# Gated attention block in fp32r: the odd tile's output sum split by inner channels, one more mirrored half of a key pair, and u's load and turn moved

## The chip, the cores and the metric

The kernel runs on one core of a Trainium2 chip. The metric is the device time of one execution in microseconds, as the median of several runs. The engines are TensorE (PE, with PEld for its weight loads), VectorE (DVE), ScalarE (ACT), GpSimd (POOL) and SyncE (SP), whose queue issues nearly all DMA transfers here.

## The reference

For eight batches of 3200 positions, with 256 channels and 64 channels for the scores:

```python
scores = scale * np.matmul(z, z.transpose(0, 2, 1))   # scale = 1 / 3200
attn = np.maximum(scores, 0.0) ** 2
x = u * np.matmul(attn, v)
gate_pre = sum over k < 5 of conv_w[k] * (x shifted by 4 - k positions)
gate = 1 / (1 + exp(-gate_pre))
out = (gate * (x @ w_val)) @ w_out
```
The weights of the attention are symmetric, since queries and keys are the same `z`.

## The kernel before

All products are made of three fp32r matmuls: each operand is split into a high and a low part (`ah`, `al` for the attention's weights, `gvh`, `gvl` for the gated values), and low x high, high x low and high x high are added in PSUM. The high part is a cast, mostly on ACT, and the low part a subtraction on DVE.

A batch has 25 tiles of 128 positions. The queries go in 7 chunks of 4, 4, 4, 4, 3, 3, 3 tiles (the last batch: 4, 4, 4, 4, 4, 3, 2); the keys in 13 pairs of tiles, of which the last is single. A *step* is one pair of one chunk, 91 steps to a batch, and the program is written step by step. In step s TensorE multiplies the values with the weights of step s (`attend`, lines 338 and 532), and makes the scores of step s + 3 (`AHEAD`), from which ACT (relu, square, cast; lines 489, 490, 492) and DVE (`al`, line 498) make that step's weights. The order on each engine is the order in which the program writes it; a table `todo` says after which step each piece of side work stands (`at_step`).

*Mirrored pairs.* Where the scores of an earlier chunk already hold the block, transposed, it isn't computed again: DVE turns blocks of the weights (`turned`, line 413, two buffers), SP writes them to DRAM (`mir`), and a later chunk fetches them (`m<-mir`, `m_fetch`, four buffers) three steps before they are cast. `mirrored` asks that both tiles of the pair are kept. Pair 9 (tiles 18 and 19) lies across chunks 4 and 5 in all batches but the last: for the queries of chunk 5, tile 18's block is kept, tile 19 is its own chunk. So far the whole pair is computed there.

*Behind the attention.* When a chunk is done, DVE multiplies the accumulators with the turned `u` (`gated`, line 562, `x<-acc,ut`). During the next chunk the convolution, the gate and the value product follow (`BEHIND`), with `gvl` of the inner channels 0 to 127 (`e = 0`) at step 8 and of 128 to 255 (`e = 1`) at step 11. At the first step of the chunk after that comes the output projection (`project`, or `project_whole` where no scores are due in the step): two banks `misc0` and `misc1`, whose even tiles go to the one and odd tiles to the other. Of the last tile of an odd chunk each bank gets half the output channels (`project_places`). ACT copies bank 0 after step 1 and bank 1 after step 2 into `ob` (`out_copy`, line 724), which SP stores.

*u.* SP loads `u` of a chunk as eight transfers in four groups, one group a step (`u_load`), and DVE turns it (`u_prep`, line 551, `ut<-u_raw`). There is one buffer of each, so a load waits until the turn of the chunk before is done. The steps are counted from the first of the chunk that it belongs to: loads begin at -6 in chunks 0, 1 and 6 and at -11 in the others, and the turn stands at 1.

Of the kernel before, what the change touches and what calls it, by code (L numbers as in the profile page):

```python
# [11 lines left out]
ALU = mybir.AluOpType  # L12
P = 128
BLK = 32
# [3 lines left out]
def attn_glu_kernel(  # L18
# [345 lines left out]
    def scores(b, c, i, terms=range(3)):  # L364
# [13 lines left out]
        for j in range(2):  # L378

            g, t = all_homes[b][k + (j if n == 2 else 0)]  # L380
            ks = slice(t * P, (t + 1) * P)
            qs = slice(0, a) if n == 2 else slice(j * (a // 2), (j + 1) * (a // 2))
            kk = zt[b, g]
            mms = []
            for m in terms:
                kp, qp = ((0, 1), (1, 0), (0, 0))[m]
                mms.append((s[:, j, : w * n // 2], kk[:, kp, ks], q[:, qp, qs], m == 0, m == 2))
            sides.append(mms)
# [9 lines left out]
    def halves(b, c, i):  # L398
        return two_pairs(b, c) and i == own(b, c, 1)

    def mirrored(b, c, i):
# [37 lines left out]
    def m_fetch(b, c, i):  # L439

        n, y = pairs[i][1], all_sizes[b][c] * BLK
        mt = m_in[b, c, i] = sb.tile([P, 2 * CW], F32, name="m", bufs=4)
        if halves(b, c, i):
            nc.sync.dma_start(mt[:, : 16 * BLK], mirror[b, c, c].rearrange("p a x -> p (a x)"))
            return
        into = mt[:, : P // BLK * n * y].rearrange("p (a x) -> p a x", x=n * y)
        for j, g, t, m in runs(b, i):
            nc.sync.dma_start(into[:, :, j * y : (j + m) * y], mirror[b, g, c][:, :, t * y : (t + m) * y])
# [6 lines left out]
    def weights_of(b, c, i):  # L455
# [5 lines left out]
        hi, lo = ah[:, : n * w], al[:, : n * w]  # L461
        if halves(b, c, i):
            s = st_.pop((b, c, i))
            a = sb.tile([P, 2 * CW], F32, name="a", bufs=2)[:, :w]
            nc.scalar.activation(a.rearrange("p (j x) -> p j x", j=2), s[:, :, : w // 2], AF.Relu, scale=scale)
            nc.scalar.activation(a, a, AF.Square)  # L466
            m = m_in.pop((b, c, i))[:, :w].rearrange("p (a j x) -> p a j x", a=P // BLK, j=2)

            his, los = (x.rearrange("p (j a h x) -> p a j h x", j=2, a=P // BLK, h=2) for x in (hi, lo))
            a = a.rearrange("p (j a x) -> p j a x", j=2, a=P // BLK)  # L470
            parts = [(m, his[:, :, :, 0], los[:, :, :, 0])]
            parts.append((a, *(x[:, :, :, 1].rearrange("p a j x -> p j a x") for x in (his, los))))
            for src, h, _ in parts:
# [188 lines left out]

    def project_places(b, c):

        n = all_sizes[b][c]
        whole, half = slice(0, D), D // 2
        banks = [[], []]
        for t in range(n - n % 2):
            banks[t % 2].append((t // 2 * D, t, whole))
        if n % 2:  # L670
            for x in range(2):
                banks[x].append((n // 2 * D, n - 1, slice(x * half, (x + 1) * half)))
        return banks

    def project_list(b, c, x, first, last):
        wh, wl = weights["out"]
        gvh, gvl = gvs[b, c]
        places = project_places(b, c)[x]
        out_ = []
        for e in range(DH):  # L680
            for p, (at_, t, ch) in enumerate(places):
                ts = slice(t * P, (t + 1) * P)
                po = pos[b, c][x][:, at_ : at_ + ch.stop - ch.start]
                for m, (gp, wp) in enumerate(((gvl, wh), (gvh, wl), (gvh, wh))):
                    out_.append(
                        (
                            po,
                            gp[:, e, ts],
                            wp[:, e, ch],
                            first and e == p == m == 0,  # L690
                            last and e == DH - 1 and p == len(places) - 1 and m == 2,
                        )
                    )
        return out_
# [24 lines left out]
    def out_copy(b, c, x, on=nc.scalar.copy):  # L719
        if x == 0:  # L720
            obs[b, c] = sb.tile([P, CW // P, D], F32, name="ob", tag=OB.get((b, c), "gvl"), bufs=1)
        ob = obs[b, c]
        for at_, t, ch in project_places(b, c)[x]:
            on(ob[:, t, ch], pos[b, c][x][:, at_ : at_ + ch.stop - ch.start])

# [24 lines left out]
    def start(b, c):  # L750
# [20 lines left out]
    Z_FROM = {b: (-12, -7, -1, 7, 17, 23, 32) if b > 1 else (22, 26, 3, 8, 17, 30, 34) for b in range(1, B)}  # L771

    CONVERSIONS = (
        (2, 2, convert_conv(), 14),
# [3 lines left out]
    for b in range(B):  # L778
        for c in range(n_chunks):
            s0 = start(b, c)  # L780
            nxt = s0 + NP
            for h in range(DH):
                for part in range(2):
                    at_step((s0 - 11 if 1 < c < n_chunks - 1 else max(s0 - 6, 2)) + 2 * h + part, u_load, b, c, h, part)
            if (b, c) != LAST:
                for r, fn, args in BEHIND:
                    at_step(nxt + r, fn, b, c, *args)
                for x in range(DH):
                    at_step(nxt + project_at(*steps[nxt][:2]) + 1 + x, out_copy_before, b, c, x)
            at_step(max(s0 + 1, 6), u_prep, b, c)  # L790

# [18 lines left out]
            for i in range(NP):  # L810
                if mirrored(b, c, i) or halves(b, c, i):
                    at_step(s0 + place[b, c, i] - AHEAD - FETCH, m_fetch, b, c, i, first=True)
# [159 lines left out]
```

## Time and profile before

| | |
|---|---|
| median of 3 runs | 2310.14 us (2309.87 to 2310.98) |
| the profiled execution | 2310.52 us, its span 2308.7 us |
| granted TensorE clock | 1.000 |
| PE, PEld, DVE, ACT busy | 100%, 87%, 78%, 77% of the span |
| DMA | 465 MB, 76.2% of 16 engines' span on SP's queue |
| chain of waits, by engine | PE 95%, ACT 2%, DVE 1%, DMA 1%, issue 1% |

The busy share of PE is that of matmuls whose ends are modelled; they are pipelined, so the time that one takes from the next is the distance between two starts, which the timeline shows. A row of the timeline gives the start, the time (of all its instructions), engine and line, the operation, tiles and shapes, and in brackets the idle time before it with what ended it. A row of waits gives who waited for whom: total us, times, longest. A row of groups gives count, total busy time and mean ns, and then the idle time before them.

### The profile page before, as it was taken

What the parts mean: (1) busy time and instruction counts of PE and PEld (TensorE: products, weight loads), DVE (VectorE), ACT (ScalarE), POOL (GpSimd) and SP (SyncE); (2) the same over time, 40 slices, a digit from 0 to 9 for tenths busy, and PEclk for the clock granted to TensorE, in tenths of its full rate; (3) what the DMA queues carried; (4) which work ended last, traced back from release to release, by engine and by line L of the source; (5) the groups of instructions that cost most, each with busy time, mean ns of one, the idle gap of its engine ahead of it and who ended that gap; (6) DMA issues with size and microseconds to landing.
All of it is one profiled execution on the core that took longest, in us unless ns stands there. A gap on an engine that the chain in (4) does not pass through costs nothing.

```text
span 2308.7 us, 47650 instructions
## 1 busy us (share of the span) xinstructions
PE 2300.3 (100%) x18845; PEld 2019.1 (87%) x18845; DVE 1810.4 (78%) x2362; ACT 1782.7 (77%) x2417; POOL 55.0 (2%) x108
## 2 busy tenths in 40 slices
PE   9999999999999999999999999999999999999999
PEld 7889988889888998889988899888998889988889
DVE  8777787787878878788788887788877888778776
ACT  8988788776888768887688776887768876687765
POOL 0000000000000000000000000000000000000000
PEclk9999999999999999999999999999999999999999
DMA  6255798778977889688896789878897788976653
GB/s 132 65 157 154 204 260 206 197 202 238 249 187 202 216 237 249 168 212 220 239 235 182 202 226 245 220 190 207 236 229 209 206 215 229 249 179 165 182 165 90
DMA packets 684881, 465.04 MB, mean 201 GB/s; under 512 B 351600, under 2 KB 635504, under 8 KB 684656
## 3 DMA queue, kind: packets, MB, share of 16 engines
q1 hardware_dynamic: 683600, 461.86, 76.2%
q8 instruction: 148, 2.42, 0.5%
q14 instruction: 77, 0.63, 0.1%
q10 hardware_dynamic: 1056, 0.13, 0.0%
HBM read 250.36 MB, written 211.48 MB: 200 GB/s over the span
## 4 chain that ended last, share of the span: by engine, by line
PE 95%; ACT 2%; DVE 1%; DMA 1%; issue 1%; SPq 0%; DVEq 0%; ACTq 0%
PE acc L338 44%; PE acc L532 29%; PE s L338 10%; PE misc L338 6%; PE misc L706 5%; PE misc L640 1%; ACT a L490 1%; DMA v_hl<-v_kept 1%; ACT a L489 1%; ACT ah L492 0%; DVE gvl L661 0%; DMA mir<-turned 0%; DVE al L498 0%; SPq L166 0%; DMA z_raw<-in_z_dram 0%
## 5 line engine op out<-in xcount | busy, mean ns | idle before, releaser
L338 PE MATMUL acc<-ah,v_hl 64*128 64x512 f32 (+1 forms) x6632 | 1073.1, 375 | 0.4 <-DVE v_hl L296 0.4
L338 PEld LDWEIGHTS acc<-ah,v_hl 64*128 64x128 f32 x6632 | 620.6, 184 | 112.6 <-issue 13.0
L532 PE MATMUL acc<-ah,v_hl 128*128 128x384 f32 (+2 forms) x2284 | 639.0, 355 | 0.1
L498 DVE TENSOR_TENSOR al<-a,ah 128x1024 fp32r<-128x1024 f32 (+3 forms) x395 | 431.1, 1092 | 260.6 <-ACT ah L492 252.3
L338 PE MATMUL acc<-al,v_hl 64*128 64x512 f32 (+1 forms) x3316 | 626.7, 374 | 0.7 <-DVE al L498 0.7
L489 ACT ACTIVATE a<-s 128x1024 f32<-128x1024 f32 (+3 forms) x395 | 362.7, 918 | 194.2 <-PE s L338 191.3
L532 PEld LDWEIGHTS acc<-ah,v_hl 128*128 128x128 f32 x2284 | 416.8, 188 | 47.5 <-ACT a L466 7.1
L498 DVE TENSOR_TENSOR al<-m,ah 128x768 fp32r<-128x768 f32 (+2 forms) x303 | 307.9, 1023 | 134.4 <-ACT ah L492 133.7
L532 PE MATMUL acc<-al,v_hl 128*128 128x384 f32 (+2 forms) x1142 | 402.2, 352 | 0.0
L490 ACT ACTIVATE a<-a 128x1024 f32<-128x1024 f32 (+3 forms) x395 | 378.3, 958 | 12.6
L492 ACT CAST ah<-m 128x768 fp32r<-128x768 f32 (+2 forms) x303 | 267.3, 892 | 147.6 <-DMA m<-mir 98.0
L338 PEld LDWEIGHTS acc<-al,v_hl 64*128 64x128 f32 x3316 | 312.7, 184 | 47.6 <-DVE al L498 1.2
L492 ACT CAST ah<-a 128x1024 fp32r<-128x1024 f32 (+2 forms) x357 | 339.4, 951 | 11.3
L413 DVE STREAM_TRANSPOSE turned<-a 128x1024 f32<-128x1024 f32 (+3 forms) x318 | 319.3, 1010 | 8.2 <-DMA mir<-turned 6.7
L603 DVE SCALAR_TENSOR_TENSOR gate<-x,cw,gate 128x512 f32<-128x512 f32 (+2 forms) x448 | 303.5, 678 | 4.4 <-ACT gate L601 0.3
L338 PE MATMUL s<-zq,zhl 64*128 64x512 f32 (+3 forms) x2052 | 261.8, 358 | 0.0
L532 PEld LDWEIGHTS acc<-al,v_hl 128*128 128x128 f32 x1142 | 214.8, 188 | 14.9 <-DVE al L498 0.2
L338 PEld LDWEIGHTS s<-zq,zhl 64*128 64x128 f32 x2052 | 185.8, 184 | 29.5
L562 DVE TENSOR_TENSOR x<-acc,ut 128x512 f32<-128x512 f32 (+2 forms) x112 | 67.5, 629 | 41.8 <-PE acc L338 26.3
L608 ACT ACTIVATE gate<-gate 128x512 f32<-128x512 f32 (+2 forms) x112 | 65.4, 583 | 34.2 <-DVE gate L603 34.1
L304 ACT CAST v_made<-v_raw 128x512 fp32r<-128x512 f32 x97 | 55.9, 576 | 40.4 <-DMA v_kept<-v_made 39.4
L706 PE MATMUL misc<-w_out_hi,gvl 128*128 128x256 f32 (+1 forms) x304 | 85.8, 282 | 0.6 <-DVE gvl L661 0.3
(114 smaller groups left out, 2020.8 us busy)
## 6 DMA issues: line engine op xcount, KB each, us to landing
m<-mir SPq DMA_DIRECT2D x191, 384.0 KB, 5.1
mir<-turned SPq DMA_DIRECT2D x340, 192.0 KB, 3.7
mir<-turned SPq DMA_DIRECT2D x188, 256.0 KB, 4.3
m<-mir SPq DMA_DIRECT2D x94, 512.0 KB, 6.0
v_hl<-v_kept SPq DMA_DIRECT2D x84, 512.0 KB, 6.7
v_kept<-v_made SPq DMA_DIRECT2D x71, 512.0 KB, 5.1
u_raw<-in_u_dram SPq DMA_DIRECT2D x264, 64.0 KB, 3.7
out_dram<-ob SPq DMA_DIRECT2D x33, 512.0 KB, 4.0
```

The source lines that it names most:

```text
L304: nc.scalar.copy(v_made[b, g, t][:, 0, :m, :], v_raw[b, g][:, t : t + m, :])
L338: ins = nc.tensor.matmul(out_, st[r], mv[r], start=first, stop=last)
L413: nc.vector.transpose(into[:, t : t + m], a[:, j * w : (j + m) * w].rearrange("p (t m x) -> p t m x", t=m, x=BLK))
L489: nc.scalar.activation(a.rearrange("p (j x) -> p j x", j=2), s[:, :, :each], AF.Relu, scale=scale)
L490: nc.scalar.activation(a, a, AF.Square)
L492: nc.scalar.copy(hi, a)
L498: nc.vector.tensor_tensor(lo, a, f32(hi), op=ALU.subtract)
L532: nc.tensor.matmul(out_, st, mv, start=first, stop=last)
L562: nc.vector.tensor_tensor(x[:, h, HALO : HALO + w], accs[b, c][h][:, :w], ut[b, c][:, h, :w], op=ALU.mult)
L603: nc.vector.scalar_tensor_tensor(g, tap, cw[:, h, k : k + 1], g, op0=ALU.mult, op1=ALU.add)
L608: nc.scalar.activation(g, g, AF.Sigmoid)
L706: nc.tensor.matmul(out_, st, mv, start=first, stop=last)
```

## The change

There are three parts.

1. The last tile of an odd chunk is projected with all 256 output channels into both banks: bank 0 gets the sum over the inner channels `e = 0`, bank 1 that over `e = 1`. ACT copies bank 0's part, and DVE adds bank 1's. The list of matmuls now also goes tile by tile within `e`.
2. Pair 9 of chunk 5 (`split`): tile 18's weights are fetched from the mirror, and only tile 19 is computed, its queries divided between the two row halves of TensorE.
3. In batches 1 to 7 `u` is loaded from -2 on in chunks 1 and 2 and from -9 in chunk 3, and turned at step 10 in chunks 0 and 1 and at step 3 in chunk 2.

```diff
+            one_tile = n == 1 or split(b, c, i)
+            g, t = all_homes[b][k + (n - 1 if one_tile else j)]
-            qs = slice(0, a) if n == 2 else slice(j * (a // 2), (j + 1) * (a // 2))
+            qs = slice(j * (a // 2), (j + 1) * (a // 2)) if one_tile else slice(0, a)
...
+    def split(b, c, i):
+        (j, g, *_), *more = runs(b, i)
+        return bool(more) and more[0][1] == c and keeps(b, g, c) and (b, c) != (B - 1, n_chunks - 1)
...
-        for j, g, t, m in runs(b, i):
+        for j, g, t, m in runs(b, i)[: 1 if split(b, c, i) else None]:
+            if split(b, c, i):
+                into = mt[:, : P // BLK * y].rearrange("p (a x) -> p a x", x=y)
...
-        if halves(b, c, i):
+        if halves(b, c, i) or split(b, c, i):
...
+            m = m_in.pop((b, c, i))[:, :w]
+            if split(b, c, i):
+                parts = [(m, hi[:, :w], lo[:, :w]), (a, hi[:, w:], lo[:, w:])]
...
-        places = project_places(b, c)[x]
+        places = [(t, e) for e in range(DH) for t in range(x, n - n % 2, 2)] + [(n - 1, x)] * (n % 2)
+        for p, (t, e) in enumerate(places):
+            ts = slice(t * P, (t + 1) * P)
+            po = pos[b, c][x][:, t // 2 * D : (t // 2 + 1) * D]
+            for m, (gp, wp) in enumerate(((gvl, wh), (gvh, wl), (gvh, wh))):
+                ends = p == len(places) - 1 and m == 2
+                out_.append((po, gp[:, e, ts], wp[:, e], first and p == m == 0, last and ends))
...
+        for t in range(x, n - n % 2, 2):
+            on(ob[:, t, :], pos[b, c][x][:, t // 2 * D : (t // 2 + 1) * D])
+        if n % 2:
+            half = pos[b, c][x][:, n // 2 * D : (n // 2 + 1) * D]
+            if x == 0:
+                nc.scalar.copy(ob[:, n - 1, :], half)
+            else:
+                nc.vector.tensor_tensor(ob[:, n - 1, :], half, ob[:, n - 1, :], op=ALU.add)
...
+    U_LOAD = ((-6, -6, -11, -11, -11, -11, -6), (-6, -2, -2, -9, -11, -11, -6))
+    U_PREP = ((1,) * n_chunks, (10, 10, 3) + (1,) * (n_chunks - 3))
...
-                    at_step((s0 - 11 if 1 < c < n_chunks - 1 else max(s0 - 6, 2)) + 2 * h + part, u_load, b, c, h, part)
+                    at_step(max(s0 + U_LOAD[b > 0][c], 2) + 2 * h + part, u_load, b, c, h, part)
...
-            at_step(max(s0 + 1, 6), u_prep, b, c)
+            at_step(max(s0 + U_PREP[b > 0][c], 6), u_prep, b, c)
```

How this moves instructions, at three places. First TensorE, the projection of chunk 4 of batch 2 at the start of chunk 6, where bank 0's list ends and bank 1's begins. Before:

```order
L706 MATMUL misc0_11564<-w_out_hi_1008,gvl_11335 128x256
L706 MATMUL misc0_11564<-w_out_lo_1009,gvh_11334 128x256
L706 MATMUL misc0_11564<-w_out_hi_1008,gvh_11334 128x256
L706 MATMUL misc0_11564<-w_out_hi_1008,gvl_11335 128x128
L706 MATMUL misc0_11564<-w_out_lo_1009,gvh_11334 128x128
L706 MATMUL misc0_11564<-w_out_hi_1008,gvh_11334 128x128
L706 MATMUL misc1_11565<-w_out_hi_1008,gvl_11335 128x256
L706 MATMUL misc1_11565<-w_out_lo_1009,gvh_11334 128x256
L706 MATMUL misc1_11565<-w_out_hi_1008,gvh_11334 128x256
```
Now:

```order
L700 MATMUL misc0_11516<-w_out_hi_1008,gvl_11285 128x256
L700 MATMUL misc0_11516<-w_out_lo_1009,gvh_11284 128x256
L700 MATMUL misc0_11516<-w_out_hi_1008,gvh_11284 128x256
L700 MATMUL misc1_11517<-w_out_hi_1008,gvl_11285 128x256
L700 MATMUL misc1_11517<-w_out_lo_1009,gvh_11284 128x256
L700 MATMUL misc1_11517<-w_out_hi_1008,gvh_11284 128x256
```
A bank had two groups of three wide and three narrow matmuls, one for each `e`; now it has three groups of three wide ones, in bank 0 for tile 0 with `e = 0`, tile 0 with `e = 1` and tile 2 with `e = 0`.

Second ACT, chunk 5 of batch 2 at pair 9. Before:

```order
L608 ACTIVATE gate_11164<-gate_11164 128x384
L492 CAST ah_11298<-m_11209 128x4x2x96
L489 ACTIVATE a_11341<-s_11314 128x768
L490 ACTIVATE a_11341<-a_11341 128x768
L492 CAST ah_11339<-a_11341 128x768
L656 CAST gvh_11334<-gv_11336 128x384
```
Now:

```order
L620 ACTIVATE gate_11112<-gate_11112 128x384
L504 CAST ah_11248<-m_11157 128x4x2x96
L473 ACTIVATE a_11291<-s_11264 128x384
L474 ACTIVATE a_11291<-a_11291 128x384
L486 CAST ah_11289<-m_11179 128x384
L486 CAST ah_11289<-a_11291 128x384
L668 CAST gvh_11284<-gv_11286 128x384
```
The two passes have half the elements, and the cast has become two of half the size, the first from the fetched block `m`.

Third DVE at the end of chunk 1 of batch 2, from the last pair's `al` (of halves) to the accumulators. Before:

```order
L652 TENSOR_TENSOR gv_9406<-misc1_9160,gate_8933 128x512
L479 TENSOR_TENSOR al_9421<-m_9253,ah_9420 128x4x2x64
L479 TENSOR_TENSOR al_9421<-a_9422,ah_9420 128x8x64
L498 TENSOR_TENSOR al_9448<-m_9305,ah_9447 128x4x2x128
L661 TENSOR_TENSOR gvl_9256<-gv_9406,gvh_9255 128x512
L562 TENSOR_TENSOR x_9473<-acc0_8899,ut_8986 128x512
```
Now:

```order
L664 TENSOR_TENSOR gv_9343<-misc1_9099,gate_8877 128x512
L491 TENSOR_TENSOR al_9358<-m_9190,ah_9357 128x4x2x64
L491 TENSOR_TENSOR al_9358<-a_9359,ah_9357 128x8x64
L563 STREAM_TRANSPOSE ut_9381<-u_raw_8746 128x1024
L510 TENSOR_TENSOR al_9387<-m_9242,ah_9386 128x4x2x128
L673 TENSOR_TENSOR gvl_9193<-gv_9343,gvh_9192 128x512
L574 TENSOR_TENSOR x_9415<-acc0_8843,ut_9381 128x512
```
The turn of chunk 1's `u` stood behind `xl` at the chunk's step 1; now it stands between the last pair's `al` and the next chunk's first. On SP the eight loads of chunk 2's `u`, which stood among the writes of chunk 1's turned blocks, now stand in a row behind the last fetch for chunk 2 and ahead of the store of an output.

More of the change, by code (lines that the diff above doesn't have):

```diff
@@ L378, in scores @@
         for j in range(2):
-            g, t = all_homes[b][k + (j if n == 2 else 0)]
+            one_tile = n == 1 or split(b, c, i)
+            g, t = all_homes[b][k + (n - 1 if one_tile else j)]
             ks = slice(t * P, (t + 1) * P)
-            qs = slice(0, a) if n == 2 else slice(j * (a // 2), (j + 1) * (a // 2))
+            qs = slice(j * (a // 2), (j + 1) * (a // 2)) if one_tile else slice(0, a)
             kk = zt[b, g]
@@ L386, in scores @@
                 kp, qp = ((0, 1), (1, 0), (0, 0))[m]
-                mms.append((s[:, j, : w * n // 2], kk[:, kp, ks], q[:, qp, qs], m == 0, m == 2))
+                mms.append((s[:, j, : w // 2 if one_tile else w], kk[:, kp, ks], q[:, qp, qs], m == 0, m == 2))
             sides.append(mms)
@@ L466, in weights_of @@
             nc.scalar.activation(a, a, AF.Square)
[L467 to L472, printed above, removed]
+            m = m_in.pop((b, c, i))[:, :w]
+            if split(b, c, i):
+                parts = [(m, hi[:, :w], lo[:, :w]), (a, hi[:, w:], lo[:, w:])]
+            else:
+                m = m.rearrange("p (a j x) -> p a j x", a=P // BLK, j=2)
+                his, los = (x.rearrange("p (j a h x) -> p a j h x", j=2, a=P // BLK, h=2) for x in (hi, lo))
+                a = a.rearrange("p (j a x) -> p j a x", j=2, a=P // BLK)
+                parts = [(m, his[:, :, :, 0], los[:, :, :, 0])]
+                parts.append((a, *(x[:, :, :, 1].rearrange("p a j x -> p j a x") for x in (his, los))))
             for src, h, _ in parts:
@@ L661, in gate_value_low, with project_list @@
         nc.vector.tensor_tensor(gvl[:, e, :w], gv_.pop((b, c, e))[:, :w], f32(gvh[:, e, :w]), op=ALU.subtract)
-    def project_places(b, c):
+    def project_list(b, c, x, first, last):
         n = all_sizes[b][c]
[L666 to L675, printed above, removed]
         wh, wl = weights["out"]
         gvh, gvl = gvs[b, c]
-        places = project_places(b, c)[x]
+        places = [(t, e) for e in range(DH) for t in range(x, n - n % 2, 2)] + [(n - 1, x)] * (n % 2)
         out_ = []
[L680 to L693, printed above, removed]
+        for p, (t, e) in enumerate(places):
[4 more added lines that the diff above has]
+                out_.append((po, gp[:, e, ts], wp[:, e], first and p == m == 0, last and ends))
         return out_
@@ L722, in out_copy @@
         ob = obs[b, c]
-        for at_, t, ch in project_places(b, c)[x]:
-            on(ob[:, t, ch], pos[b, c][x][:, at_ : at_ + ch.stop - ch.start])
+        n = all_sizes[b][c]
+        for t in range(x, n - n % 2, 2):
[4 more added lines that the diff above has]
+                nc.scalar.copy(ob[:, n - 1, :], half)
+            else:
+                nc.vector.tensor_tensor(ob[:, n - 1, :], half, ob[:, n - 1, :], op=ALU.add)
     def out_store(b, c):
@@ L810, in attn_glu_kernel @@
             for i in range(NP):
-                if mirrored(b, c, i) or halves(b, c, i):
+                if mirrored(b, c, i) or halves(b, c, i) or split(b, c, i):
                     at_step(s0 + place[b, c, i] - AHEAD - FETCH, m_fetch, b, c, i, first=True)
```

## The prediction

> **What bounds the kernel now.** I read the page first (busy shares, chain of waits), then TensorE's waits, then the timeline at the places that the change touches.
>
> ```profile
> PE 2300.3 (100%) x18845; PEld 2019.1 (87%) x18845; DVE 1810.4 (78%) x2362; ACT 1782.7 (77%) x2417; POOL 55.0 (2%) x108
> ```
> ```profile
> PE acc L338 <- DVE al L498: 0.7, 1, 0.7
> ```
> ```profile
> PEld misc L706 <- DVE gvl L661: 2.1, 7, 0.5
> ```
> PE is busy for 2300.3 of 2308.7 us. A busy PE need not be fast, so I looked at who holds it up: the second row (TensorE's waits) shows that a late `al` holds a matmul once in the whole run, and the third that a late `gvl` holds a weight load seven times, 2.1 us in sum. Starts of matmuls follow one another by their own length almost everywhere. So time goes or comes by what TensorE itself has to issue, as long as DVE, ACT and the transfers keep their lead.
>
> **The odd tile's projection.** An odd chunk (three tiles) has 12 matmuls of 256 columns and 12 of 128 columns now, and 18 of 256 after the change. First one whole projection row by row, up to the start of what follows it, then an even chunk's from the chain of waits (24 matmuls of 256).
>
> ```profile
> 841.28 0.28 PE L706 MATMUL misc<-w_out_hi,gvl 128*128 128x256 f32 x1
> ...
> 841.63 0.22 PE L706 MATMUL misc<-w_out_hi,gvl 128*128 128x128 f32 x1
> 841.69 0.28 PE L706 MATMUL misc<-w_out_lo,gvh 128*128 128x128 f32 x1
> 841.80 0.27 PE L706 MATMUL misc<-w_out_hi,gvh 128*128 128x128 f32 x1
> 841.91 0.33 PE L706 MATMUL misc<-w_out_hi,gvl 128*128 128x256 f32 x1
> 842.09 0.28 PE L706 MATMUL misc<-w_out_lo,gvh 128*128 128x256 f32 x1
> ...
> 843.97 0.39 PE L532 MATMUL acc<-ah,v_hl 128*128 128x384 f32 x1
> ```
> ```profile
> 398.81 2.87 PE misc L706 x24
> ```
> From start to start a 256-column matmul takes 0.12 us (0.35 for the first three). The three of 128 columns take 0.06, 0.11 and 0.11, and the wide one behind them 0.18 in place of 0.12: the narrow ones are no cheaper than a wide one in practice. The whole takes 843.97 - 841.28 = 2.69 us. Eighteen wide ones at 2.87/24 = 0.1196 take 2.15. Saved: 0.54 per odd chunk.
>
> Where the projection runs on the two row halves at once, the timeline shows the same:
>
> ```profile
> 875.39 0.28 PE L338 MATMUL misc<-w_out_hi,gvl 64*128 64x256 f32 x2
> ...
> 876.71 0.45 PE L338 MATMUL s<-zq,zhl 64*128 64x512 f32 x2
> 877.00 0.33 PE L338 MATMUL misc<-w_out_hi,gvl 64*128 64x256 f32 x2
> ...
> 878.37 0.44 PE L338 MATMUL acc<-ah,v_hl 64*128 64x512 f32 x2
> ```
> 1.32 + 1.37 = 2.69 us again. How many there are follows from the groups of matmuls by form:
>
> ```profile
> L338 PE MATMUL misc<-w_out_hi,gvl 64*128 64x128 f32 x112 | 12.5, 219 | 0.0
> ```
> ```profile
> L706 PE MATMUL misc<-w_out_hi,gvl 128*128 128x128 f32 x32 | 7.1, 221 | 0.0
> ```
> A whole projection has 4 narrow matmuls with `gvl`, one on halves has 8, so 32/4 + 112/8 = 8 + 14 = 22 odd chunks. **Term 1: 22 x 0.54 = 11.9 us less.** The last of them (2296.64) lies straight ahead of the final chunk's value matmuls, so it counts too.
>
> A rule bears on this. The Trainium skill, TensorE: Matmul & The Clock Gate, section "Back-to-back issue gap", gives an isolated gap of N/2.4 + 2.5 ns, which is 56 ns for 128 columns and 109 for 256; by it 12 narrow ones cost what 6 wide ones cost, and term 1 would be an estimated 0.3 us in place of 11.9. The rows of 0.11 us do not agree with it. The page's section "LDWEIGHTS" puts a load of 128 columns at 107 ns, and with that they agree.
>
> The other side of term 1: the two sums are now added by one DVE instruction of 256 elements that reads PSUM, 22 times, while ACT loses two short copies and gains one of 256. The nearest row reads PSUM too:
>
> ```profile
> L562 DVE TENSOR_TENSOR x<-acc,ut 128x256 f32<-128x256 f32 x2 | 0.8, 420 | 1.0 <-PE acc L532 1.0
> ```
> That is 22 x 0.42 = 9.2 us of DVE. It stands at step 2 of a chunk, ahead of the `al` that TensorE needs at step 5. In chunk 1, the tightest of the three kinds that get it, that `al` ends 2.3 us before its first use:
>
> ```profile
> 653.75 1.22 DVE L498 TENSOR_TENSOR al<-a,ah 128x1024 fp32r<-128x1024 f32 x1 [0.68 <-ACT ah L492]
> ```
> ```profile
> 657.29 0.39 PE L338 MATMUL acc<-al,v_hl 64*128 64x512 f32 x2
> ```
> Since the turn of `u` (1.23 us) leaves the same stretch, I take nothing. Without cover it would be 9.2 us.
>
> A shorter projection is also a shorter cover: it runs while DVE empties the accumulators that the next chunk writes. At the start of chunk 6 the first of them is free at
>
> ```profile
> 842.19 0.55 DVE L562 TENSOR_TENSOR x<-acc,ut 128x384 f32<-128x384 f32 x1
> ```
> 842.74, and TensorE writes it at 843.97 (above). Of these 1.23 us, 0.54 go; 0.7 stay, so again nothing.
>
> **The pair across two chunks.** Seven times (batches 0 to 6, chunk 5, pair 9) six score matmuls of 384 columns become six of 192. Both sizes are in the trace, with the start of what follows:
>
> ```profile
> 826.66 0.68 PE L338 MATMUL s<-zq,zhl 64*128 64x384 f32 x6
> 827.18 0.33 PE L338 MATMUL acc<-ah,v_hl 64*128 64x384 f32 x2
> ```
> ```profile
> 834.46 0.47 PE L338 MATMUL s<-zq,zhl 64*128 64x192 f32 x6
> 834.77 0.36 PE L338 MATMUL acc<-ah,v_hl 64*128 64x384 f32 x2
> ```
> 0.52 against 0.31, **term 2: 7 x 0.21 = 1.5 us less.** ACT does two passes on half the elements and casts in two pieces; DVE subtracts in two pieces, some 0.1 us more. The seven added fetches of 192 KB are issued three steps ahead. One that came late would hold ACT first, and TensorE only beyond the lead of that pair's `al`, which ends at 830.93 and is used at 833.59:
>
> ```profile
> 829.97 0.96 DVE L498 TENSOR_TENSOR al<-a,ah 128x768 fp32r<-128x768 f32 x1 [3.83 <-ACT ah L492]
> ```
> ```profile
> 833.59 0.33 PE L338 MATMUL acc<-al,v_hl 64*128 64x384 f32 x2
> ```
> A lead of 2.7 us; I take nothing for the fetches.
>
> **u late.** For batches 1 to 7 the turn of `u` moves from step 1 to step 10 in chunks 0 and 1, from 1 to 3 in chunk 2, and the loads of chunks 1, 2 and 3 by 4, 9 and 2 steps. What DVE does around step 10 now:
>
> ```profile
> 632.81 1.23 DVE L498 TENSOR_TENSOR al<-m,ah 128x1024 fp32r<-128x1024 f32 x1 [1.63 <-ACT ah L492]
> ...
> 680.83 1.23 DVE L498 TENSOR_TENSOR al<-m,ah 128x1024 fp32r<-128x1024 f32 x1 [1.48 <-ACT ah L492]
> ```
> Directly ahead of these two (ends of chunks 0 and 1) DVE idles 1.63 and 1.48 us, and the moved turn of 1.23 stands exactly there: it costs nothing. In chunk 2 the loads are issued from about 686 on, where SP is idle (rows under rival C), for some 4 us, and land 3.7 us after issue (median on the page), at about 694. The turn now stands at
>
> ```profile
> 693.16 1.24 DVE L551 STREAM_TRANSPOSE ut<-u_raw 128x1024 f32<-128x1024 f32 x1
> ```
> and goes two steps, some 7 us, later: in time. Where the turn left in chunk 0, it frees time at the one `al` that TensorE waits for:
>
> ```profile
> 317.89 1.25 DVE L413 STREAM_TRANSPOSE turned<-a 128x1024 f32<-128x1024 f32 x1 [3.16 <-DMA mir<-turned]
> ...
> 319.90 1.23 DVE L551 STREAM_TRANSPOSE ut<-u_raw 128x1024 f32<-128x1024 f32 x1
> ...
> 321.49 1.22 DVE L498 TENSOR_TENSOR al<-a,ah 128x1024 fp32r<-128x1024 f32 x1
> ```
> ```profile
> 322.76 0.50 PE L338 MATMUL acc<-al,v_hl 64*128 64x512 f32 x2 [0.75 <-DVE al L498]
> ```
> Without the turn this `al` comes 1.2 us sooner. **Term 3: 0.8 us less** (the idle 0.75 and a slower restart), bounds 0 and 0.9.
>
> Sum: 11.9 + 1.5 + 0.8 = 14.2. The profiled execution took 2310.5 (2308.7 of span, 1.8 around it), so 2296.3; the median of the timed runs lies 0.4 lower, so **2295.9**.
>
> **Rivals.**
>
> *A: gvl of the second half comes late.* In the new order bank 0 reaches `e = 1` after three matmuls (0.36 us), so far after six (0.63). At the start of chunk 6 that `gvl` is just done, and at the start of chunk 5 (an even projection) it is the wait of the seven rows above:
>
> ```profile
> 841.12 0.55 DVE L661 TENSOR_TENSOR gvl<-gv,gvh 128x384 fp32r<-128x384 f32 x1
> ```
> It ends at 841.67, 0.39 us into the projection; TensorE would want it at 0.36. For it: that is late by 0.03 and a handshake, and the seven waits now cost 2.1/7 = 0.3 us each. Against it: chunk 5 is where the split pair takes work off ACT, which is busy nearly without a break from that pair to the end of the chunk. ACT's first pass on 768 and on 384 elements:
>
> ```profile
> 827.38 0.81 ACT L489 ACTIVATE a<-s 128x768 f32<-128x768 f32 x1 [4.21 <-PE s L338]
> ...
> 835.99 0.48 ACT L489 ACTIVATE a<-s 128x384 f32<-128x384 f32 x1
> ```
> 0.33 less on each of two passes, against 0.2 for the second piece of the cast: some 0.5, while TensorE gains 0.21. So `gvl` should come at about 0.39 - 0.5 + 0.21 = 0.1. Price if ACT's gain is lost: 0.39 + 0.21 - 0.36 = 0.24 late and some 0.14 of handshake and restart, 0.4 each, 7 times, 2.7 us: **2298.6**. Chance 0.13.
>
> *B: narrow matmuls cost only their columns*, and the 0.11 us comes from something else that stays (the accumulation in one bank, say). Then terms 2 and 3 alone remain: 2310.1 - 2.3 = **2307.8**. For it is only the first narrow one's 0.06. Chance 0.05.
>
> *C: u's loads block SP's queue, slower.* Eight issues now stand in a row at the ends of chunks 0 and 1, behind a wait for DVE's turn; the writes of the turned blocks are queued behind them, and a late write holds DVE as at 317.89. SP in chunk 2 now, and the issue time of two loads:
>
> ```profile
> 685.47 0.52 SPq L448 DMA_DIRECT2D m<-mir  x1
> 696.20 0.41 SPq L729 DMA_DIRECT2D out_dram<-ob  x1
> ...
> 700.36 0.99 SPq L166 DMA_DIRECT2D u_raw<-in_u_dram  x2
> ```
> Eight take 4.0 us. If all of it reached DVE, less the 2.3 us of lead, it is 1.7 us at each of 14 places, 24 us: **2320**. It decides from 14.2/14 = 1.0 us a place on. Against it: SP issues nothing from 686.0 to 696.2, just where the eight will stand. Chance 0.03.
>
> **How the numbers follow.** Forecast 0.79, A 0.13, B 0.05, C 0.03. The forecast's own range is 2294.5 to 2297.5 (term 3 at nothing, term 1 by 0.05 a chunk). With A, and half of the DVE adds' price showing in two of three kinds of chunk (some 3 us), the range is 2294.3 to 2300.8. A measurement of this kernel tells about 0.2%, 4.6 us, from no change: faster by that is forecast and A (0.92), B is no change (0.05), C slower (0.03).
>
> **What would show it.** Right: an odd projection of 2.15 us, in both forms; the split pair's scores in 0.31; `ut` of chunks 0 and 1 in DVE's idle time just before the last `al` of the chunk, with no wait for its transfer; no PE wait at batch 1, chunk 0; DVE's `ob` add not in the chain. Wrong: waits of `misc` for `gvl` more than seven (A), odd projections near 2.6 without a wait (B), or PE waiting for `al` again, with `turned` waiting for `mir` in chunks 1 and 2 (C).

## The result, and the profile after

| | before | changed |
|---|---|---|
| median of the timed runs | 2310.01 us (2309.74 to 2310.98, 4 runs) | 2297.18 us (2296.48 to 2297.72, 4 runs) |
| ratio | | 0.9944, 95% interval 0.9926 to 0.9961 |
| profiled execution, its span | 2310.52, 2308.7 us | 2296.48, 2294.7 us |
| last matmul starts at | 2304.54 us | 2290.41 us |

The change is 12.8 us faster by the medians and 14.0 by the two profiled executions; 14.2 was forecast, and 2295.9 as the time. In a later comparison on one chip the changed kernel had 2297.07 (5 runs) against 2310.32 for the kernel before.

The code has moved by some lines: 706 is now 700 (`project_whole`), 498 is 510 (`al`), 413 is 419 (`turned`), 435 is 441 (writes of turned blocks), 661 is 673 (`gvl`), 551 is 563 (`ut`), and the store is line 730. The first row of the page and the two rows of TensorE's waits that answer to those of before:

```profile
PE 2287.3 (100%) x18629; PEld 2009.2 (88%) x18629; DVE 1817.6 (79%) x2391; ACT 1777.5 (77%) x2402; POOL 54.7 (2%) x108
```
```profile
PE misc L700 <- DVE gvl L673: 0.3, 1, 0.3
```
```profile
PEld misc L700 <- DVE gvl L673: 2.1, 7, 0.5
```
There are 216 matmuls fewer, TensorE is still the engine that sets the end, its wait for `al` is gone, and the seven late `gvl` are the same seven. The timeline of TensorE, first an odd projection in one piece (up to the matmul behind it), then one on the two row halves, then the scores of the split pair:

```profile
836.81 0.28 PE L700 MATMUL misc<-w_out_hi,gvl 128*128 128x256 f32 x1
...
838.83 0.28 PE L700 MATMUL misc<-w_out_hi,gvh 128*128 128x256 f32 x1
838.95 0.34 PE L544 MATMUL acc<-ah,v_hl 128*128 128x384 f32 x1
```
```profile
870.32 0.28 PE L338 MATMUL misc<-w_out_hi,gvl 64*128 64x256 f32 x2
...
871.39 0.39 PE L338 MATMUL s<-zq,zhl 64*128 64x512 f32 x2
871.62 0.38 PE L338 MATMUL misc<-w_out_hi,gvl 64*128 64x256 f32 x2
...
872.78 0.40 PE L338 MATMUL acc<-ah,v_hl 64*128 64x512 f32 x2
```
```profile
829.99 0.47 PE L338 MATMUL s<-zq,zhl 64*128 64x192 f32 x6
830.30 0.36 PE L338 MATMUL acc<-ah,v_hl 64*128 64x384 f32 x2
```
The first takes 2.14 us (2.69 before). The second takes 2.46 with the two score matmuls in its middle; the same stretch took 878.37 - 875.39 = 2.98 before. The split pair's scores take 0.31. With 8 projections of the first kind and 14 of the second, 8 x 0.55 + 14 x 0.52 = 11.7 us.

I also added up, over the whole trace, the distance from each matmul's start to the next one's, by kind of matmul. From before to after: the projection 10.7 less, the scores 2.3 less, the attention's products 1.4 less, the rest 0.3 more; together the 14.1 us by which the last start moved. (Where two scores stand in the middle of a projection, they start faster too; so some 0.8 of the 11.7 counts as scores here.)

The turn of `u` at the end of chunk 1 stands where DVE was idle for 1.48 us:

```profile
674.97 1.24 DVE L563 STREAM_TRANSPOSE ut<-u_raw 128x1024 f32<-128x1024 f32 x1
676.53 1.22 DVE L510 TENSOR_TENSOR al<-m,ah 128x1024 fp32r<-128x1024 f32 x1 [0.33 <-ACT ah L504]
```
One row had grown, and it led to what follows. It is the group of DVE's big transpositions on the page:

```profile
L419 DVE STREAM_TRANSPOSE turned<-a 128x1024 f32<-128x1024 f32 (+3 forms) x318 | 320.0, 1011 | 22.3 <-DMA mir<-turned 21.2
```
Before:

```profile
L413 DVE STREAM_TRANSPOSE turned<-a 128x1024 f32<-128x1024 f32 (+3 forms) x318 | 319.3, 1010 | 8.2 <-DMA mir<-turned 6.7
```
The waits for the writes to DRAM had been 6.7 us in sum (8.2 with all idle time). TensorE did not feel them here.

### The profile page after: what moved, and what is told of

It is laid out like the page before. It is cut to its first block, busy times and chain, and to the rows that moved or that the text cites. A ratio compares the mean times of both kernels' runs of the same rounds, so it can differ in the third digit from the quotient of the medians.

```text
span 2294.7 us, 47249 instructions
## 1 busy us (share of the span) xinstructions
PE 2287.3 (100%) x18629; PEld 2009.2 (88%) x18629; DVE 1817.6 (79%) x2391; ACT 1777.5 (77%) x2402; POOL 54.7 (2%) x108
## 4 chain that ended last, share of the span: by engine, by line
PE 94%; ACT 2%; SPq 1%; DVE 1%; issue 1%; DMA 1%; ACTq 0%; DVEq 0%
PE acc L338 44%; PE acc L544 28%; PE s L338 10%; PE misc L338 6%; PE misc L700 4%; PE misc L652 1%; SPq L166 1%; ACT a L502 1%; ACT a L501 1%; ACT ah L504 0%; SPq L280 0%; DMA m<-mir 0%; DVE gvl L673 0%; DVE al L510 0%; DMA u_raw<-in_u_dram 0%
## 5 line engine op out<-in xcount | busy, mean ns | idle before, releaser
L510 DVE TENSOR_TENSOR al<-a,ah 128x1024 fp32r<-128x1024 f32 (+3 forms) x388 | 424.1, 1093 | 222.8 <-ACT ah L504 215.0
L501 ACT ACTIVATE a<-s 128x1024 f32<-128x1024 f32 (+3 forms) x388 | 357.2, 921 | 152.2 <-PE s L338 149.1
L502 ACT ACTIVATE a<-a 128x1024 f32<-128x1024 f32 (+3 forms) x388 | 372.3, 960 | 12.3
L338 PEld LDWEIGHTS acc<-al,v_hl 64*128 64x128 f32 x3316 | 314.2, 184 | 45.4
L504 ACT CAST ah<-a 128x1024 fp32r<-128x1024 f32 (+3 forms) x350 | 333.6, 953 | 11.1
L419 DVE STREAM_TRANSPOSE turned<-a 128x1024 f32<-128x1024 f32 (+3 forms) x318 | 320.0, 1011 | 22.3 <-DMA mir<-turned 21.2
L668 ACT CAST gvh<-gv 128x512 fp32r<-128x512 f32 (+2 forms) x112 | 64.0, 572 | 26.6 <-DVE gv L664 26.4
```

Of the source, the lines that this page charges most:

```text
L338: ins = nc.tensor.matmul(out_, st[r], mv[r], start=first, stop=last)
L419: nc.vector.transpose(into[:, t : t + m], a[:, j * w : (j + m) * w].rearrange("p (t m x) -> p t m x", t=m, x=BLK))
L504: nc.scalar.copy(hi, a)
L510: nc.vector.tensor_tensor(lo, a, f32(hi), op=ALU.subtract)
L668: nc.scalar.copy(gvs[b, c][0][:, e, :w], gv_[b, c, e][:, :w])
```

## The experiments

Each kernel was compared with the kernel before on the same chip; the interval of such a ratio is 0.08 to 0.15% to either side, 2 to 3.5 us. Smaller differences below rest on the starts in the traces or on ranges of runs that don't overlap. Each kernel has line numbers of its own; the tiles tell what a row is.

### Each part alone

Three kernels have one part of the change each, on the kernel before; a fourth run is the change itself. The projection alone (with `project_list`, `project_whole` and the copies as in the change):

```diff
+        places = [(t, e) for e in range(DH) for t in range(x, n - n % 2, 2)] + [(n - 1, x)] * (n % 2)
...
+                nc.vector.tensor_tensor(ob[:, n - 1, :], half, ob[:, n - 1, :], op=ALU.add)
```


> Only the odd tile's projection is split by inner channels; the pair across two chunks and u stay as before. Theory 1 (TensorE issues 6 matmuls fewer, the three parts are independent): the 22 odd projections take 10.8 us less, so about 10.8 below the kernel before, and the idle 0.75 at the `al` of batch 1 chunk 0 is still there. Theory 2 (the parts meet at chunk 6's start: without the lighter pair ACT and DVE hand over the `gvl` of the second half about 0.3 us later, while TensorE wants it 0.27 earlier): seven weight loads at chunk 6's start wait some 0.2 to 0.4 us each, the saving is 8 to 9.4, and the list of weight-load waits for `gvl` has 14 in place of 7. Rival B (narrow matmuls cost their columns): no more than 1 us.

The pair alone:

```diff
+    def split(b, c, i):
...
+            one_tile = n == 1 or split(b, c, i)
```


> Only the pair across two chunks is split; projection and u as before. Theory 1 (scores' columns): seven times 0.21 us, 1.5 below the kernel before, the scores of that pair 0.31 from start to start. Theory 2 (a few tenths more, if `gvl` at chunk 6's start also comes earlier and a wait goes there): 1.5 to 2.5 below. Rival (seven added fetches come late or crowd the queue): 0 to 3 above.

`u` alone:

```diff
+    U_LOAD = ((-6, -6, -11, -11, -11, -11, -6), (-6, -2, -2, -9, -11, -11, -6))
+    U_PREP = ((1,) * n_chunks, (10, 10, 3) + (1,) * (n_chunks - 3))
```


> Only u's loads and its turn are moved; projection and pair as before. Theory 1 (one wait for `al` goes, nothing else changes): 0.8 below the kernel before. Theory 2 (the moved turn and loads cost the lead of `al` in chunks 2 and 3 but TensorE feels none of it): the same 0.8, with the waits of `turned` for `mir` at some 20 us in place of 6.7. Rival C: above the kernel before, with TensorE waiting for `al` in chunks 1 to 3.

> The changed kernel as it is, beside its three parts on the same chip. If the parts are independent their savings add up to its own (some 13 to 14 us); if the projection alone saves less by more than 1 us, the pair's split pays twice.

| kernel | median (runs) | from the kernel before, 2310.32 | ratio, interval |
|---|---|---|---|
| projection alone | 2312.29 (11) | **+2.0** | 1.0009, 1.0000 to 1.0017 |
| pair alone | 2309.06 (11) | -1.3 | 0.9995, 0.9986 to 1.0004 |
| u alone | 2309.87 (11) | -0.5 | 0.9999, 0.9990 to 1.0008 |
| all three | 2297.07 (5) | **-13.3** | 0.9942, 0.9929 to 0.9954 |

The parts add up to +0.2, and together they make -13.3. The pair and `u` came out about as my first theory had it (1.5 and 0.8), though neither is clear of its interval. For the projection both my theories fell: it was to bring 8 to 11 us, and brought nothing (2.0 slower, with an interval that begins at no change), although its matmuls are as short as in the change. What it gains in the projection it loses at the attention's products (11.4 us more from start to start). Its DVE waits say why:

```profile
DVE turned L413 <- DMA mir<-turned: 45.7, 26, 3.9
```
Here is batch 2, chunk 1 of the projection-only kernel, whose projection starts at 636.51. First SP's queue (each row: start, issue time of all its transfers, how many), then DVE, then TensorE:

```profile
652.43 0.41 SPq L718 DMA_DIRECT2D out_dram<-ob  x1
652.88 1.20 SPq L166 DMA_DIRECT2D u_raw<-in_u_dram  x2
654.12 3.21 SPq L435 DMA_DIRECT2D mir<-turned  x4
657.38 3.38 SPq L166 DMA_DIRECT2D u_raw<-in_u_dram  x4
660.87 0.42 SPq L320 DMA_DIRECT2D v_kept<-v_made  x1
661.39 3.84 SPq L435 DMA_DIRECT2D mir<-turned  x4
665.27 2.42 SPq L166 DMA_DIRECT2D u_raw<-in_u_dram  x2
667.73 0.64 SPq L444 DMA_DIRECT2D m<-mir  x1
```
```profile
651.99 0.42 DVE L713 TENSOR_TENSOR ob<-misc,ob 128x256 f32<-128x256 f32 x1
...
664.95 0.71 DVE L413 STREAM_TRANSPOSE turned<-a 128x512 f32<-128x512 f32 x1
669.57 0.71 DVE L413 STREAM_TRANSPOSE turned<-a 128x512 f32<-128x512 f32 x1 [3.91 <-DMA mir<-turned]
...
681.02 0.68 DVE L479 TENSOR_TENSOR al<-a,ah 128x512 fp32r<-128x512 f32 x1
```
```profile
681.76 0.50 PE L532 MATMUL acc<-al,v_hl 128*128 128x512 f32 x1 [0.74 <-DVE al L479]
```
Read it from the top. The store of the odd chunk's output can be issued only when DVE has added the two sums (651.99 + 0.42). In the kernel before, it waited for ACT's copy:

```profile
650.12 0.41 SPq L729 DMA_DIRECT2D out_dram<-ob  x1
```
That is 12.9 us after the start of the chunk's projection (637.23 there); now it is 652.43 - 636.51 = 15.9. Behind it in the queue stand loads of `u` and writes of turned blocks, and from there on SP issues almost without a break: eight loads of `u` take 1.20 + 3.38 + 2.42 = 7.0 us of it. So the delay isn't made up; the writes are late, the `turned` buffer that DVE needs at 665.66 is not free, and it stands for 3.91 us, with the `al` of the next steps behind. At the chunk's end TensorE waits. The Trainium skill, TensorE: Matmul & The Clock Gate, says in its table of specifications that VectorE's queue is strictly first in, first out. The trace agrees: for 3.91 us DVE does nothing, with the gated values and the next `al` behind.

A smaller thing shows in the same trace. The projection-only kernel at the start of chunk 6:

```profile
842.52 0.28 PE L688 MATMUL misc<-w_out_hi,gvl 128*128 128x256 f32 x1
...
844.86 0.34 PE L532 MATMUL acc<-ah,v_hl 128*128 128x384 f32 x1
```
2.34 us in place of 2.14. On DVE:

```profile
842.36 0.55 DVE L661 TENSOR_TENSOR gvl<-gv,gvh 128x384 fp32r<-128x384 f32 x1
```
Without the lighter pair `gvl` of the second half is done 0.39 us into the projection, where TensorE wants it at 0.36, and that costs 0.2 us. That is rival A, in the kernel that lacks what was said to hold it off.

### One part taken away

`u` left as before, and then the pair left as before (each the change without one part; the diffs are those above with the signs turned).

```diff
-    U_LOAD = ((-6, -6, -11, -11, -11, -11, -6), (-6, -2, -2, -9, -11, -11, -6))
-    U_PREP = ((1,) * n_chunks, (10, 10, 3) + (1,) * (n_chunks - 3))
```


> The change without its last part: projection and pair split, u as before. The projection alone came out 2.0 us above the kernel before, with `turned` waiting 45.7 us for `mir` (6.7 before) and `al` late for TensorE at chunk 1's end, so u's move seems to be the condition of the gain. Theory 1 (u's move is the condition, in chunks 0 to 2): some 2309 to 2312, 12 to 14 above the change, `turned` again waiting over 35 us. Theory 2 (the pair's split is the condition, since it relieves ACT): 2298 to 2299, u's move worth its own 0.8.

```diff
-            one_tile = n == 1 or split(b, c, i)
+            one_tile = n == 1
```


> The change without the pair's split: projection split and u moved. Theory 1 (u's move is the condition): 1.5 above the change if the pair's split is worth only its score columns (2298.6), 2.5 to 4 above if the lighter pair also keeps `gvl` in time at chunk 6's start (rival A's price, 0.24 to 0.4 at seven places). Theory 2 (the pair's split is the condition): 2308 to 2312.

Without `u`'s move: 2309.18 (11 runs; ratio 0.9995, 0.9986 to 1.0004), 12.1 above the change, with 43.9 us of `turned` waiting for `mir`. Without the split of the pair: 2299.20 (5 runs; 0.9951, 0.9938 to 0.9964), 2.1 above. So the move of `u`, worth 0.5 us or nothing by itself, is in this change the condition of nearly the whole gain. The pair is worth its scores and the 0.2 us of `gvl` at chunk 6: its odd projections there took 2.35 us again.

### Is it the queue, or DVE's work?

The move of `u` takes a transposition from DVE and eight issues from SP's queue in the same stretch, so it doesn't say which of the two counts. Two kernels do. The first is the change without `u`'s move, and the store is issued one step later, so that fewer writes stand behind it:

```diff
-            if x == DH - 1:
-                out_store(*divmod(b * n_chunks + c - 1, n_chunks))
...
+                if b or c:
+                    at_step(nxt + project_at(*steps[nxt][:2]) + 3, out_store, *divmod(b * n_chunks + c - 1, n_chunks))
```


> As the change without u's move, and the store of a chunk's output is issued one step later (behind the next writes of turned blocks, in place of ahead of u's loads and those). In the projection-only kernel the store waits for DVE's add of the two halves (issued at 652.43 in batch 2 chunk 1, by its distance from the same chunk's `al` 3.4 us later than before), and the loads of u and the writes of turned blocks stand behind it. Theory Q (the store's new wait for DVE blocks SP's queue, late writes then hold DVE's `turned`, and that holds `al`): most of the gain comes back without u's move, 2297 to 2301, and `turned` waits for `mir` fall below 25 us. Theory D (the add and u's turn are too much work for DVE in the same steps, the queue only shows it): stays at 2308 to 2312.

The second is the kernel before, with one short copy per odd chunk moved from ACT to DVE, so that its store has the wait, while the projection and `u` stay as they were:

```diff
-            on(ob[:, t, ch], pos[b, c][x][:, at_ : at_ + ch.stop - ch.start])
+            odd = x == 1 and t == all_sizes[b][c] - 1 and all_sizes[b][c] % 2
+            (nc.vector.tensor_copy if odd else on)(ob[:, t, ch], pos[b, c][x][:, at_ : at_ + ch.stop - ch.start])
```


> The kernel before, with one edit: of the odd tile's two copies into `ob` the second (bank 1, 128 channels) is done by DVE in place of ACT, so the store of an odd chunk waits for DVE as it does behind the add, while the projection keeps its 24 matmuls and its length. Theory Q (the wait of the store for DVE is enough): 5 to 14 above the kernel before, `turned` waiting over 30 us for `mir`. Rival (it takes the shorter projection too, which gives DVE and SP 0.54 us less per chunk): within 2 us of the kernel before.

The first took 2297.96 (5 runs; 0.9946, 0.9933 to 0.9959): 11.2 of the 12.1 us came back with no work taken from DVE. The second took 2319.12 (5 runs; 1.0037, 1.0023 to 1.0052), 8.8 us slower than the kernel before. Its copies are

```profile
652.85 0.28 DVE L725 COPY ob<-misc 128x128 f32<-128x128 f32 x1
```
of 0.28 us, 22 x 0.28 = 6.2 us in all: it lost more than the work that DVE was given. Its queue shows the cause again, and the kernel with the later store shows the cure (same batch and chunk):

```profile
653.16 0.41 SPq L730 DMA_DIRECT2D out_dram<-ob  x1
653.62 1.19 SPq L166 DMA_DIRECT2D u_raw<-in_u_dram  x2
654.85 3.27 SPq L435 DMA_DIRECT2D mir<-turned  x4
```
```profile
647.42 0.85 SPq L166 DMA_DIRECT2D u_raw<-in_u_dram  x2
649.68 3.29 SPq L441 DMA_DIRECT2D mir<-turned  x4
653.07 1.11 SPq L728 DMA_DIRECT2D out_dram<-ob  x1
654.23 3.38 SPq L166 DMA_DIRECT2D u_raw<-in_u_dram  x4
```
With the wait in the old place, four writes are issued from 654.85 on, 17.8 us after the start of that kernel's projection (637.10); with the store behind them, from 649.68, 14.7 us after it (635.00). And in the change itself the store is about as late as in the projection-only kernel, 648.85 - 633.47 = 15.4 us after the projection's start, but no load of `u` stands behind it:

```profile
648.85 0.41 SPq L730 DMA_DIRECT2D out_dram<-ob  x1
649.31 3.63 SPq L441 DMA_DIRECT2D mir<-turned  x4
653.05 1.10 SPq L320 DMA_DIRECT2D v_kept<-v_made  x1
655.30 4.25 SPq L441 DMA_DIRECT2D mir<-turned  x4
```
One table for all kernels, of the same batch and chunk, from the starts of single instructions in the traces. Times are counted from the start of the chunk's projection; the last `turned` is the one that waited 3.91 us above.

| kernel | store issued | that `turned` starts | median |
|---|---|---|---|
| before | 12.9 | 29.4 | 2310.0 to 2310.3 |
| pair alone | 12.9 | 29.4 | 2309.1 |
| u alone | 12.9 | 29.4 | 2309.9 |
| projection alone | 15.9 | 33.1 | 2312.3 |
| projection and pair, u as before | 15.7 | 31.9 | 2309.2 |
| before, a copy on DVE | 16.1 | 33.1 | 2319.1 |
| projection and pair, store later | 18.1 | 30.7 | 2298.0 |
| projection and u | 15.4 | 29.3 | 2299.2 |
| the change | 15.4 | 29.4 | 2297.1 |
| the change, longer add (below) | 16.7 | 31.2 | 2301.7 |
| the change, `gvl` early (below) | 15.4 | 29.4 | 2293.5 |
| the same, store later (below) | 17.8 | 28.8 | 2293.6 |

It isn't how late the store is that goes with the time, but how late DVE gets its buffer back. From about 31 us on TensorE feels it.

The traces say the same chunk by chunk. From the start of chunk 1's projection to that of chunk 2's it is 45.4 us in the kernels with the shorter projection, 46.0 with the old one and 46.2 with the widened one (below), where nothing waits. Batches 1 to 6 of fourteen traces, one of each kernel and a second of the change, give 84 such stretches. Where that `turned` starts by 31.0 us, none is more than 0.1 us longer. Where it starts later, every one is: by 0.5 at 31.2 us, 1.2 at 31.7 and 2.5 at 33.1 with the shorter projection, by 1.0 at 32.2 and 2.0 at 33.2 with the copy on DVE. In sum the six stretches lose 11.7 us in the projection alone, 10.6 in the kernel without `u`'s move and 9.1 with the copy on DVE. So most of the harm lies in one chunk of six batches, and not at all 22 odd projections.

The later store left 0.9 us to the change, with ranges of runs that overlap. The longest wait that its trace has beyond the change's is for `al` in batch 1, chunk 0, 1.3 us: the place of term 3.

### How much the cover holds

Three copies of 256 elements on DVE ahead of each add, in the changed kernel:

```diff
+                for _ in range(3):
+                    nc.vector.tensor_copy(spare, half)
                 nc.vector.tensor_tensor(ob[:, n - 1, :], half, ob[:, n - 1, :], op=ALU.add)
```


> The changed kernel, and at each of the 22 places three copies of 256 elements out of PSUM stand on DVE ahead of the add of the two halves, about 0.42 us each: 22 x 1.26 = 28 us more of DVE, and the store of the output waits 1.26 longer. If the lead of `al` and the room in SP's queue still cover that (my reading of the change): within 1 of the change, 2297 to 2298. If the cover is used up: several us above, with `turned` waiting more than 35 us for `mir` and TensorE waiting for `al`; all of it felt would be 2325.

```profile
649.76 1.33 DVE L728 COPY spare<-misc 128x256 f32<-128x256 f32 x3
651.01 0.42 DVE L729 TENSOR_TENSOR ob<-misc,ob 128x256 f32<-128x256 f32 x1
```
2301.70 (4 runs; 0.9965, 0.9951 to 0.9979), 4.6 above the change, between my two cases. Of 22 x 1.25 = 27.5 us more before the add, about a sixth reached the end. By the starts it lies in four chunks with waits for `al`: 1.9 us in batch 1, chunk 0, 0.5 and 0.4 in batch 2, chunks 1 and 3, and 1.7 in batch 5, chunk 3. Only the second is of the kind in the table. No copy stands in or just before a chunk 3, and the kernel with `gvl` early (below) has such a wait there too (0.5 us, batch 3), so how the others hang together with the copies is not shown. The add's own 0.42 us is covered with something to spare; with four times that the kernel is slower.

### What a narrow matmul costs

The kernel before, with its 128-column matmuls widened to 256 (the odd tile is computed whole in both banks, and half of each is left unused):

```diff
-                banks[x].append((n // 2 * D, n - 1, slice(x * half, (x + 1) * half)))
+                banks[x].append((n // 2 * D, n - 1, whole))
```


> The kernel before, with the 12 matmuls of 128 columns of each odd projection widened to 256: both banks get the odd tile's whole product, and half of each is left unused (the same output, twice the work for that tile). If a 128-column matmul costs its weight load (0.11 against 0.12 from start to start): 2.87 in place of 2.69 per odd projection, 22 x 0.18 = 4 above the kernel before. If it cost its columns (rival B): 12 x 0.053 x 22 = 14 above.

```profile
841.07 0.28 PE L706 MATMUL misc<-w_out_hi,gvl 128*128 128x256 f32 x1
...
843.93 0.34 PE L532 MATMUL acc<-ah,v_hl 128*128 128x384 f32 x1
```
2313.47 (10 runs; 1.0015, 1.0006 to 1.0025), 3.5 above the kernel before, where the second case had 14. Twelve matmuls of twice the columns cost 2.86 - 2.69 = 0.17 us here. A matmul of 128 columns costs nearly what one of 256 does, and rival B is out. The Trainium skill, TensorE: Matmul & The Clock Gate, section "LDWEIGHTS", has a formula by which a load of 128 weight columns takes an estimated 107 ns. The narrow matmul agrees: at 2.86/24 = 0.119 us for a wide one, it is (2.69 - 12 x 0.119)/12 = 0.105. (By the starts the projections became 5.1 us longer in sum, some more than my 4; 2.7 of it came back elsewhere: 0.8 at scores, and 1.9 at the attention's products, where this trace has no matmul waiting for the one late `al`.)

### The seven waits that were left

The chain of the change's seven late `gvl` (chunk 3's, at the start of chunk 5) is short: on DVE it stands behind an `al` for which DVE first waits 0.71 us.

```profile
802.67 0.96 DVE L510 TENSOR_TENSOR al<-m,ah 128x768 fp32r<-128x768 f32 x1 [0.71 <-ACT ah L504]
803.54 0.69 DVE L673 TENSOR_TENSOR gvl<-gv,gvh 128x512 fp32r<-128x512 f32 x1
```
The projection starts at 803.35. One step earlier it stands ahead of that `al`:

```diff
+                    early = c == 3 and b < B - 1 and args == (1,) and fn is gate_value_low
-                    at_step(nxt + r, fn, b, c, *args)
+                    at_step(nxt + r - early, fn, b, c, *args)
```


> The changed kernel, and in batches 0 to 6 the `gvl` of the second half that belongs to chunk 3 is subtracted one step earlier (so it stands ahead of the `al` of that step on DVE, in its idle 0.7 us, and not behind). Theory (the seven weight-load waits left at chunk 5's start, 0.32 us each from start to start, are felt by TensorE in full): 2.2 below the change, 2295.0. Rival (the time goes to the `al` behind it on DVE, which is then late): within 0.5 of the change or above it.

And the same with the later store:

> The same with the store of a chunk's output issued one step later as well, behind the next writes of turned blocks. Theory Q says the store's wait for DVE no longer holds TensorE once u is moved: the same time as with the `gvl` edit alone (2295.0, within 0.5), while the waits of `turned` for `mir` fall from 21 to 27 us to below 20. If part of them is still felt: up to 1 below.

DVE in the kernel with `gvl` early, ahead of the projection at 801.78:

```profile
799.73 0.65 DVE L673 TENSOR_TENSOR gvl<-gv,gvh 128x512 fp32r<-128x512 f32 x1
800.29 0.70 DVE L196 STREAM_TRANSPOSE zz<-z_raw 128x512 f32<-128x512 f32 x1
801.10 0.96 DVE L510 TENSOR_TENSOR al<-m,ah 128x768 fp32r<-128x768 f32 x1
```
`gvl` is done 1.4 us ahead of the projection in place of 0.9 behind its start, and the idle 0.71 is gone too. The projection of chunk 3 takes 2.87 us in all seven batches (3.19 to 3.40 in the change). It runs in 2293.51 us (2293.04 to 2294.85, 5 runs; 0.9929, 0.9917 to 0.9942), below every run of the change: the fastest version here, 16.5 below the kernel before. With the later store as well it is 2293.56, the same, with 16.1 us of `turned` waits in place of 22.5: what is left of those waits isn't felt. The gain is 3.6 us by the medians where 2.2 was expected; by the starts, the projection accounts for 2.5, and where the rest comes from is open.

One candidate shows in the second profiled execution of the change itself, but not in the first. Batch 1, start of chunk 0:

```profile
304.29 0.33 PE L338 MATMUL misc<-w_out_hi,gvh 64*128 64x256 f32 x2
306.09 0.39 PE L338 MATMUL misc<-w_out_hi,gvl 64*128 64x256 f32 x2 [1.48 <-DVE gvl L673]
```
TensorE waits 1.5 us there for `gvl` of the second half, once in the run, and the projection takes 4.26 us in place of 2.51. This is rival A's wait, at a place of which the prediction didn't think; the two profiled executions differ by 2297.53 - 2296.48 = 1.05 us. It begins with a transfer, for which ACT waits:

```profile
298.94 0.62 ACT L304 CAST v_made<-v_raw 128x512 fp32r<-128x512 f32 x1 [1.51 <-DMA v_raw<-in_v_dram]
```
ACT's part of that `gvl` stands behind this cast. The cast starts 5.1 us ahead of the projection here, and 7.5 in the first execution. Of all traces with the shorter projection, the four in which it starts 7.5 us or more ahead have no such wait; in the others the projection is longer, by 0.2 us at 6.6, 0.5 at 6.3, 0.8 at 6.0, 1.1 at 5.8 and 1.8 at 5.1.

## Why the prediction was right, point by point

The time was forecast as 2295.9 (range 2294.3 to 2300.8) and is 2297.2. The number was right, and one of its steps rested on less than it seemed to. (The ends of the wide range don't follow from the terms: 2298.6 for rival A with the 3 us of the adds would be 2301.6.)

- **Term 1, 11.9 us: right.** 0.55 in one piece and 0.52 on the row halves make 11.7.
- **The DVE add at nothing: right for the whole change, and the step that failed as reasoned.** I weighed the add's 9.2 us against the 2.3 us of lead that `al` has, and took the turn of `u` that leaves the same stretch as a further margin. What counts is not DVE's time but that the output's store now waits for DVE, with the loads of `u` and the writes of turned blocks behind it on SP's queue. That `u`'s move, which takes these loads away, stood in the same change was luck as far as my reasoning goes. Without `u`'s move that costs 12.1 us (9.2 was my price without cover), and even 6.2 us of DVE work placed ahead of the store cost 8.8. I had asked of each added wait who is queued behind it on its engine, but not for the store, since its own time costs nothing.
- **Term 2, 1.5 us: right** in its scores (0.31 as forecast; alone 1.3 by the medians). The split is worth 2.1 in the whole, since it also holds off rival A at chunk 6.
- **Term 3, 0.8 us: the wait is gone, but its cause is open.** `u`'s move alone brought 0.5 by the medians, which is within its interval, and the last matmul start of its profile is 1.1 earlier. But no matmul waits for that `al` either in the pair alone, in the kernel before with a copy on DVE or in the one with widened matmuls, and there `u` is turned where it was. What differs is how long `turned` waits for `mir` just ahead: 3.16 us in the kernel before, 0.4 to 2.4 in these three. In the pair alone:

```profile
317.05 1.25 DVE L419 STREAM_TRANSPOSE turned<-a 128x1024 f32<-128x1024 f32 x1 [0.43 <-DMA mir<-turned]
...
320.65 1.21 DVE L510 TENSOR_TENSOR al<-a,ah 128x1024 fp32r<-128x1024 f32 x1
```
With one profile of the kernel before, it isn't shown whether `u`'s move took the wait away or whether it comes and goes.

- **The sum as a sum of parts: wrong.** The terms were treated as independent. Alone, the three parts make +0.2 us, together -13.3.
- **Late fetches at nothing, the shorter cover at nothing: right,** no wait of TensorE in the change goes back to either.
- **Rival A** didn't come where it was placed: `gvl` lands 0.13 us into the projection of chunk 6 (0.1 forecast). Its argument against, the lighter pair, is shown by the kernels without the split, where the price is 0.2 us each, half of the 0.4 that I gave it (of which no row had shown the 0.14 for handshake and restart). It did come once, at the start of batch 1, in the second profile.
- **Rival B** is out, by the 2.14 us and by the widened matmuls.
- **Rival C** had the right queue and the wrong cause. Loads of `u` and writes of turned blocks do crowd each other on SP's queue, and the waits of `turned` for `mir` rose from 6.7 to 21.2 us; but `u`'s move relieves that queue behind the store in the chunks where it was tight, and the harm is in the kernel without it.
- **The gain by medians, 12.8 where 14.2 was forecast:** the profiled execution, from which the sum was made, gained 14.0 but is also the fastest of the change's four runs. The late `gvl` of batch 1, by how late a transfer of `v` lands, is one thing that differs from execution to execution; whether it is all of it is not shown.

## What to carry to other kernels

When work moves from one engine to another, look up who waits for its result, and above all which transfers: a store that nobody is in a hurry for can hold a queue whose later entries somebody needs. Parts of a change that look independent can be each other's condition, so take each away from the whole as well as trying it alone; a part worth half a microsecond or nothing by itself carried twelve here. And a late operand on a full engine is often a matter of the order on the engine that makes it: one instruction moved by one step, in seven batches, brought 3.6 us.

## What was not expected of the hardware

- A few microseconds for which SP's queue stood were not made up for, since what followed was full. In the projection-only kernel the DMA engines were busy for 0.05 of the time from 644 to 652 us, while SP's queue stood at the store, and for 0.85 from 652 to 668. In these 16 us SP issued nearly without a break, 0.6 to 1.2 us for a load of `u` and 0.8 to 0.96 for a write of turned blocks. Whether the issuing or the DMA engines set the pace there is not shown; that the order in the queue counts is, by the 11.2 us that a store one step later gave back.
- Work added to DVE cost from a sixth of its duration (27.5 us added before the store, 4.6 at the end) to 1.4 times its duration (6.2 added, 8.8 at the end), by what stood behind it on another engine's queue.
